# Keys and queries loaded further ahead, and the second layer's weights fetched in quarters, in a fused attention and soft-MoE kernel

## The chip, the cores and the metric

One core of one Trainium2 chip runs the whole kernel. The metric is the device time of one execution in microseconds (us), the median of several runs; lower is better.

## The reference

Three stages follow each other; the result of each is the input of the next. Shapes: q, k, v (4, 8, 1152, 64); phi (512, 32); w1 (8, 512, 1024); w2 (8, 1024, 512); w_in (512, 2048); w_out (2048, 512).

```python
# 1. attention, 4 batches x 8 heads, the queries pooled by pairs
q_pool = q.reshape(B, H, S // 2, 2, D).mean(axis=3)          # 576 queries, 1152 keys
attn = softmax(q_pool @ k.T / sqrt(D)) @ v                   # row sum + 1e-9
x = attn.transpose(0, 2, 1, 3).reshape(2304, 512)
# 2. soft mixture of 8 experts with 4 slots each
logits = x @ phi                                             # 2304 x 32
d = softmax(logits, over tokens); c = softmax(logits, over slots)
slot_out[e] = relu((d.T @ x)[e] @ w1[e]) @ w2[e]
x = c @ slot_out                                             # 2304 x 512, of rank 32
# 3. second layer
h = x @ w_in
g = h where h >= 1, 0 where h <= -1, (h + 1)^2 / 4 between
out = g @ w_out                                              # 2304 x 512
```

## The kernel before, in words

**Attention.** The 32 heads are taken in 16 pairs P, and the 1152 keys of a pair in 9 chunks. One chunk of one pair is a group g = 9P + c, and a group has two slots, one for each head. In each slot TensorE (PE) makes the scores (`st`, L371), ScalarE (ACT) their exponential `e` (L376), PE the product with the values (`acc`, L401), and PE and VectorE (DVE) the row maximum that a later pair needs (`mx` L305, `mp` L317). All other work, such as loading and preparing a later pair, is put into named slots by a table: `plan(P)` calls `at(group, slot, function, ...)`, and the program is written out group after group. Each engine runs its instructions in that order, and so does SP, the queue that issues all DMAs of the stage: an issue that must wait holds up all behind it.

Preparing pair P: `load_k2` and `load_q` fetch keys and queries (`kf` two issues, `qf` four), `prep_khi` (ACT, L252) and `prep_klo` (DVE) split the keys into two f16 parts in `kn`, `prep_qp`, `prep_qhi` and `prep_qlo` pool and split the queries (`qn`), `xpose_k` and `xpose_q1` are DMA transposes into `K1` and `q1`, and `dup_q1` (L291) copies q1 to the other 64 partitions. `qf` has one buffer: a pair's queries can be fetched only when `prep_qlo` of the pair before has read it. The row maxima of pair P are computed on PE (`mx`) from group 9P - 11 on, and they read K1 and q1 with its copy. The places of these steps relative to b = 9P are the two rows of the table `PREP`, in the order load, khi, klo (half groups), qp (half groups), qhi, qlo (half groups):

```python
PREP = (-20, -18, (-34, -33), -36, -16, -30), (-24, -22, (-41, -37), -41, -19, -37)
```

Row 0 is used for P = 2, row 1 for P from 3 on. Between these steps, w_out and w_in are unpacked: a piece is loaded (`f`), turned into `wst` and written to the DRAM copies `wo_dr` and `wi_dr`.

**Mixture.** Logits and softmax over tokens run along with attention. Then 32 tiles of 1 MB with halves of w1 and w2 pass through a ring of buffers on the SP queue: `h` (L775), `ht` (L784, a PE transpose), `s2o` (L827).

**Second layer.** As x = c · slot_out, h is computed as c · M with M = slot_out · w_in (32 rows). M is summed on PE from four tiles `wi`, each with 128 rows of w_in and all 2048 columns (L924). PE multiplies in f32r, so operands are split into a high part (a copy by ACT) and a low part (a subtraction): `Mhi` and `Mlo`, `ghi` and `glo` (GpSimd, which the profile calls POOL), `whi` and `wlo` (L905, L907). `w_split` makes those of w_out, and its subtractions are on POOL for 10 of the 16 row blocks and on DVE for 6. `Mrep` spreads M over the partitions (L948). Then a block of 256 tokens (n) goes through four quarters (qd) of w_in's columns: `h_unit` makes h and clips it (`cl`), `g_unit` forms g in `r`, `g_split` its two parts, and `o_part` multiplies with w_out in 12 matmuls per quarter and half block. For the first block `first_unit` and `o_first` do the same in smaller steps; units are numbered from there.

Of the kernel before, what the change touches and what calls it, by code (L numbers as in the profile page):

```python
# [13 lines left out]
ALU = mybir.AluOpType  # L14
# [18 lines left out]
LGT = 30, 31, 32, 33, 34, 36, 37  # L33
LPT = 6
WPH = 3
REA = 0
# [4 lines left out]
ADD = ((4, 1, 0, 0, 2), (5, 1, 1, 0, 1), (6, 1, 1, 1, 2), (6, 2, 0, 0, 2), (7, 2, 1, 0, 2), (8, 3, 0, 0, 1), (9, 3, 0, 1, 2),  # L41
       (10, 3, 1, 0, 2), (10, 4, 0, 0, 1), (11, 4, 0, 1, 2), (12, 4, 1, 0, 1), (13, 4, 1, 1, 2))

PREP = (-20, -18, (-34, -33), -36, -16, -30), (-24, -22, (-41, -37), -41, -19, -37)


@with_exitstack
def fused_kernel(ctx: ExitStack, tc: tile.TileContext, q, k, v, phi, w1, w2, w_in, w_out, out):
# [59 lines left out]
    wlist += [("wi", dc, 0) for dc in range(4)]  # L108
    wo_dr = dr_p.tile([128, 16, DM], F32, name="wo_dr")
    wi_dr = dr_p.tile([4, 128, DFF], F32, name="wi_dr")  # L110
    wt = {}
    nloaded, gone = 0, set()

    def w_load():
        nonlocal nloaded
        i = nloaded
        nloaded += 1
        kind, e, x = wlist[i]
        if i == NSL:
            t = x_p.tile([128, NTT * DM], F32, tag="xn", name="w1_last")[:, 0:2048]  # L120
        else:
            sl = i if i < NSL else (i - NSL - 1) % NWL
            t = wslot[sl].tile([128, 2048], F32, tag=f"w{sl}", name=f"{kind}_{e}_{x}")
        if kind == "w1":
            src = w1[e, :, x * 512:(x + 1) * 512].rearrange("(c p) f -> p c f", p=128)
            vw = t.rearrange("p (c f) -> p c f", c=4)
        elif kind == "w2":
            src = w2[e, x * 512:(x + 1) * 512, :].rearrange("(c p) d -> p c d", p=128)
            vw = t.rearrange("p (c d) -> p c d", c=4)
        else:  # L130
            src, vw = wi_dr[e], t
        if i < len(wlist) - 1:
            nc.sync.dma_start(out=vw, in_=src)
        else:

            for hf in range(2):
                a, b = [y.rearrange("p (j n) -> p j n", j=4)[:, :, hf * 256:hf * 256 + 256] for y in (vw, src)]
                nc.sync.dma_start(out=a, in_=b)
        wt[kind, e, x] = vw

    def w_used(*keys):
# [51 lines left out]
    def cv_step(n, i):  # L193
        t, dst = cv[n]
        d = dst.bitcast(I32)
        if i == 0:

            nc.vector.tensor_scalar(out=dst, in0=dst, scalar1=CLO, scalar2=CHI, op0=ALU.max, op1=ALU.min)
        elif i == 1:
            nc.vector.tensor_scalar(out=d, in0=d, scalar1=3, scalar2=0x3fffffff,  # L200
                                    op0=ALU.logical_shift_left, op1=ALU.bitwise_and)
        elif i == 2:
            nc.vector.scalar_tensor_tensor(out=d, in0=t[:, :, 1], scalar=-0x40000000, in1=d,
                                           op0=ALU.bitwise_and, op1=ALU.bitwise_or)
# [379 lines left out]
    def plan(P):  # L584
        b = NK * P
        if P > 1:
            lk, hk, lok, aq, hq_, loq = PREP[P > 2]
            for h in range(2):
                at(b + lk, 0, (load_k2, load_q)[h], P)
                at(b + hk, h, prep_khi, P, h)  # L590
                at(b + lok[h] // 2, lok[h] % 2, prep_klo, P, h)
                at(b - 17, h, xpose_k, P, h)
            at(b + aq // 2, aq % 2, prep_qp, P)
            at(b + hq_, 0, prep_qhi, P)
            at(b - 16, 0, xpose_q1, P)
# [58 lines left out]
    with tc.manual_schedule():  # L654
# [126 lines left out]
        def ht_mm(i):  # L781
            htp[i] = sc_tile("ht0")[:, 0, :] if i == 0 else hp_tile("ht1")
            for kc in range(4):
                nc.tensor.transpose(out=htp[i][:, kc * 128:(kc + 1) * 128], in_=h1s[i][:, kc * 128:(kc + 1) * 128],  # L784
                                    identity=ident)
# [24 lines left out]
        def c_xpose(n):  # L810
            for i in range(2):
# [79 lines left out]
        for hl in range(2):  # L891
            for j in range(4):
                for r in range(4):
                    src = ident[:, 32 * j:32 * j + 32] if r // 2 == hl else zcol.to_broadcast([128, 32])
                    nc.gpsimd.tensor_copy(Sel[:, hl, j, 32 * r:32 * r + 32], src)
        for e in range(E_):
            s2o(e, 1)
        pieces = [(0, 2), (2, 4), (4, 8), (8, 12), (12, 16)]
        for f0, f1 in pieces:
            nc.sync.dma_start(out=wlo[:, f0:f1, :].bitcast(F32), in_=wo_dr[:, f0:f1, :])  # L900


        def w_split(f0, f1):
            for f in range(f0, f1):
                nc.scalar.activation(out=whi[:, f, :], in_=wlo[:, f, :].bitcast(F32), func=AF.Copy)  # L905
                eng = nc.gpsimd if f < 4 or f % 2 else nc.vector
                eng.tensor_tensor(out=wlo[:, f, :], in0=wlo[:, f, :].bitcast(F32), in1=whi[:, f, :].bitcast(F32),  # L907
                                  op=ALU.subtract)

        nc.vector.tensor_copy(S2sb, s2)  # L910
        c_xpose(0)
# [4 lines left out]
        Mp = [po_tile(f"M{i}")[:, 0:DM // 2] for i in range(2)]  # L916
        wps = po_tile("warm_o")
        for dc in range(4):
            if dc < 2:
                c_xpose(1 + dc)  # L920
            for i in range(2):
                for j in range(4):
                    c0 = j * 512 + i * 256
                    nc.tensor.matmul(Mp[i][32 * j:32 * j + 32], lhsT=soT[:, dc, :],  # L924
                                     rhs=wt["wi", dc, 0][:, c0:c0 + 256], start=(dc == 0), stop=(dc == 3))
        Mst = x_p.tile([128, NTT * DM], F32R, tag="xn", name="Mst")
        Mhi, Mlo = Mst[:, DFF:DFF + DM], Mst[:, DFF + DM:DFF + 2 * DM]
        HF = [slice(0, DM // 2), slice(DM // 2, DM)]
        for i, sl in enumerate(HF):
            nc.scalar.activation(out=Mhi[:, sl], in_=Mp[i], func=AF.Copy)  # L930
            nc.vector.tensor_tensor(out=Mlo[:, sl], in0=Mp[i], in1=Mhi[:, sl].bitcast(F32), op=ALU.subtract)

        w_split(0, 2)
        wx.close()


        g_p = ctx.enter_context(tc.tile_pool(name="g", bufs=6))
# [3 lines left out]
        NBK = NT // TB  # L941
        ghi, glo, hq = {}, {}, {}

        def Mrep(j, parts):
            for i, sl in enumerate(parts):
                ps = hp_tile(f"Mr{j}_{i}")[:, 0:sl.stop - sl.start]
                for hl, src in enumerate((Mhi, Mlo)):
                    nc.tensor.matmul(ps, lhsT=Sel[:, hl, j, :], rhs=src[:, sl], start=(hl == 0), stop=(hl == 1))  # L948
                dst = Mst[:, j * 512 + sl.start:j * 512 + sl.stop]
                if (i + j) % 2 == 0:  # L950
                    nc.vector.tensor_copy(dst, ps)
                else:
                    nc.scalar.activation(out=dst, in_=ps, func=AF.Copy)


        def h_unit(n, qd, j0, j1):
# [32 lines left out]
        units = [(n, qd, 0, 4) for n in range(NBK) for qd in range(4)][2:]  # L989

        def unit_step(i):
            if i < len(units):
# [58 lines left out]

        pos = o_tiles(0)
        warm_o(WARM[3])
        Mrep(0, HF)
        for f in range(5):
            if f == 4:
                warm_o(WARM[4])
            first_unit(f)
            if f == 1:
                Mrep(1, [slice(0, DM)])  # L1060
                w_split(2, 4)
        nu = 0

        def ahead(n):
            nonlocal nu
# [4 lines left out]
        for n in range(NBK):  # L1070
            if n:
                pos = o_tiles(n)
            if n < NBK - 1:
                for qd in range(4):
                    if n == 0 and qd == 0:
                        for f in range(4):
                            o_first(0, pos, f)
                            if f < 2:
                                first_unit(5 + f)
                                Mrep(2 + f, [slice(0, DM)])  # L1080
                            if f == 1:
                                w_split(4, 8)
                            ahead(FIRST[f])
# [50 lines left out]
```

## Time and profile before

| | before |
|---|---|
| time, median of 3 runs | 782.35 us (782.05 to 782.71) |
| profiled execution, its own time | 787.7 us |
| its span | 785.9 us |
| mean granted TensorE clock | 0.983 |
| PE busy | 757.1 us, 96% |
| DVE busy | 581.4 us, 74% |
| ACT busy | 451.7 us, 57% |
| POOL busy | 125.9 us, 16% |

The page of the profile cuts the span into 40 slices of 19.6 us. Each digit is a busy share in tenths, PEclk is the granted clock in tenths:

```profile
PE   7779999999999999999999999999789999999998
DVE  6878999988989888999988793151697777666520
PEclk8889999999999999999999999999989999999999
DMA  8786788797788797799998836799600000000000
```

PE works in nearly every slice. Its low digits stand at the start (slices 1 to 3) and about two thirds of the way (slices 29 and 30), where the mixture ends and the second layer starts; the clock is below 9 tenths in the same places.

### The profile page before, as it was taken

What the parts mean: (1) busy time and instruction counts of PE and PEld (TensorE: products, weight loads), DVE (VectorE), ACT (ScalarE), POOL (GpSimd) and SP (SyncE); (2) the same over time, 40 slices, a digit from 0 to 9 for tenths busy, and PEclk for the clock granted to TensorE, in tenths of its full rate; (3) what the DMA queues carried; (4) which work ended last, traced back from release to release, by engine and by line L of the source; (5) the groups of instructions that cost most, each with busy time, mean ns of one, the idle gap of its engine ahead of it and who ended that gap; (6) DMA issues with size and microseconds to landing.
All of it is one profiled execution on the core that took longest, in us unless ns stands there. A gap on an engine that the chain in (4) does not pass through costs nothing.

```text
span 785.9 us, 19049 instructions
## 1 busy us (share of the span) xinstructions
PE 757.1 (96%) x7896; PEld 556.6 (71%) x7896; DVE 581.4 (74%) x947; ACT 451.7 (57%) x855; POOL 125.9 (16%) x100
## 2 busy tenths in 40 slices
PE   7779999999999999999999999999789999999998
PEld 6557777766767766777766776633578888888887
DVE  6878999988989888999988793151697777666520
ACT  4246667676657565676675666401686777556620
POOL 7000000000000000000000000002574444443330
PEclk8889999999999999999999999999989999999999
DMA  8786788797788797799998836799600000000000
GB/s 215 201 174 137 182 193 205 206 248 200 186 233 203 183 260 164 188 263 180 212 263 134 222 96 237 269 333 395 241 0 28 28 28 20 7 28 28 27 28 28
DMA packets 138263, 127.11 MB, mean 162 GB/s; under 512 B 80576, under 2 KB 100288, under 8 KB 137408
## 3 DMA queue, kind: packets, MB, share of 16 engines
q1 hardware_dynamic: 138176, 125.89, 61.0%
q8 instruction: 62, 1.02, 0.6%
q14 instruction: 25, 0.20, 0.1%
HBM read 87.10 MB, written 13.11 MB: 128 GB/s over the span
## 4 chain that ended last, share of the span: by engine, by line
PE 60%; DMA 2%; DVE 2%; ACT 2%; issue 1%; SPq 0%; ACTq 0%; DVEq 0%
PE acc L401 9%; PE st L371 9%; PE po L1031 8%; PE po L1032 8%; PE po L1033 8%; PE mx L305 4%; PE acc L394 3%; DMA wi<-wi_dr 2%; PE h L968 2%; PE h L775 2%; PE tx L439 1%; PE tb L466 1%; DVE r L1021 1%; PE tr L428 1%; PE lp L482 0%
## 5 line engine op out<-in xcount | busy, mean ns | idle before, releaser
L376 ACT ACTIVATE e<-st 128x576 f32<-128x576 f32 x288 | 187.0, 651 | 139.0 <-PE st L371 125.6
L317 DVE TENSOR_REDUCE mp<-mx 128x1 f32<-128x576 f32 x282 | 212.1, 754 | 44.9 <-PE mx L305 38.0
L401 PE MATMUL acc<-e,vf 128*64 128x288 f32 x1152 | 195.1, 411 | 0.5 <-ACT e L376 0.5
L305 PE MATMUL mx<-K,q 128*64 128x288 f16 x1152 | 124.8, 298 | 9.6 <-DVE mp L317 3.4
L371 PE MATMUL st<-q,K 128*64 128x288 f16 x1152 | 122.0, 288 | 5.9 <-ACT e L376 4.7
L371 PE MATMUL st<-q,S 128*64 128x288 f16 x1152 | 122.0, 287 | 0.0
L305 PEld LDWEIGHTS <-q 128*64 128x64 f16 x1152 | 66.3, 112 | 70.2 <-issue 24.5
L1031 PE MATMUL po<-whi,ghi 128*128 128x512 f32 (+1 forms) x280 | 108.5, 388 | 0.0
L1032 PE MATMUL po<-wlo,ghi 128*128 128x512 f32 (+1 forms) x280 | 108.5, 388 | 0.0
L1033 PE MATMUL po<-whi,glo 128*128 128x512 f32 (+1 forms) x280 | 108.0, 386 | 0.0
L981 DVE TENSOR_TENSOR r<-cl,r 128x1024 f32<-128x1024 f32 x34 | 80.6, 2372 | 36.9 <-ACT cl L980 36.9
L987 POOL TENSOR_TENSOR glo<-r,ghi 128x1024 fp32r<-128x1024 f32 x34 | 82.2, 2417 | 95.3 <-ACT ghi L986 95.3
L401 PEld LDWEIGHTS acc<-e,vf 128*64 128x64 f32 x1152 | 77.4, 137 | 8.3 <-ACT e L376 2.0
L371 PEld LDWEIGHTS <-K 128*64 128x64 f16 x1152 | 68.3, 110 | 20.9 <-issue 12.7
L752 POOL MEMSET xfer<- 128x1024 f32 x1 | 1.0, 957 | 493.5 <-PE pb L562 493.5
L384 DVE TENSOR_TENSOR es<-es,e 128x288 f32<-128x288 f32 (+1 forms) x144 | 77.5, 550 | 2.2 <-ACT e L376 2.2
L371 PEld LDWEIGHTS <-S 128*64 128x64 f16 x1152 | 69.3, 110 | 3.4
L971 ACT ACTIVATE r<-h,cols 128x512 f32<-128x512 f32 x68 | 43.0, 685 | 31.4 <-PE h L968 31.4
L1033 PEld LDWEIGHTS po<-whi,glo 128*128 128x128 f32 x280 | 53.2, 190 | 10.8
L1031 PEld LDWEIGHTS po<-whi,ghi 128*128 128x128 f32 x280 | 53.4, 191 | 9.8
L1032 PEld LDWEIGHTS po<-wlo,ghi 128*128 128x128 f32 x280 | 53.3, 190 | 9.3
L972 DVE TENSOR_SCALAR cl<-h 128x512 f32<-128x512 f32 x68 | 43.8, 685 | 15.8 <-ACT r L971 13.9
(191 smaller groups left out, 854.1 us busy)
## 6 DMA issues: line engine op xcount, KB each, us to landing
w<-in_moe_w_dram SPq DMA_DIRECT2D x31, 1024.0 KB, 7.9
vf<-in_v_dram SPq DMA_DIRECT2D x16, 576.0 KB, 6.1
kf<-in_k_dram SPq DMA_DIRECT2D x30, 288.0 KB, 4.1
f<-in_moe_w_out_dram SPq DMA_DIRECT2D x16, 512.0 KB, 5.1
f<-in_moe_w_in_dram SPq DMA_DIRECT2D x16, 512.0 KB, 5.5
qf<-in_q_dram SPq DMA_DIRECT2D x30, 256.0 KB, 4.9
S<-K SPq DMA_DIRECT2D x16, 288.0 KB, 5.6
out_dram<-ob SPq DMA_DIRECT2D x17, 256.0 KB, 2.0
```

What stands on the lines that cost most here:

```text
L305: nc.tensor.matmul(ps[p0:p1, i, 0:HQ], lhsT=q1[P][:, t, p0:p1], rhs=kk[:, j * HQ:(j + 1) * HQ], start=True, stop=True)
L317: nc.vector.tensor_reduce(out=mp[P][:, t, a:a + 1], in_=ps[:, :, 0:HQ], op=ALU.max, axis=AX.XY)
L371: nc.tensor.matmul(ps[c0:c0 + 64, i, 0:HQ], lhsT=kk[:, ci, c0:c0 + 64], rhs=f[:, sl[i]], start=first, stop=not first)
L376: nc.scalar.activation(out=e, in_=ps[:, :, 0:HQ], func=AF.Exp, scale=ESC)
L384: nc.vector.tensor_tensor(out=Es[P, n, h][:, i0:i1], in0=a[:, i0:i1], in1=b[:, i0:i1], op=ALU.add)
L401: nc.tensor.matmul(acc[P, i][h * 64:(h + 1) * 64, 0:HQ], lhsT=vt[P][:, h, c, :], rhs=E[P, c, h][:, i, :], start=(c == 0), stop=(c == NK - ...
L972: nc.vector.tensor_scalar(out=cl[:, a:b], in0=src, scalar1=-1.0, scalar2=1.0, op0=ALU.max, op1=ALU.min)
L981: nc.vector.tensor_tensor(out=r[:, sl], in0=cl[:, sl], in1=r[:, sl], op=ALU.add)
L987: nc.gpsimd.tensor_tensor(out=glo[n, qd][:, sl], in0=r[:, sl], in1=ghi[n, qd][:, sl].bitcast(F32), op=ALU.subtract)
L1031: nc.tensor.matmul(po, lhsT=ghi[n, qd][:, j, sl], rhs=whi[:, f, cs], start=(f == 0), stop=False)
L1032: nc.tensor.matmul(po, lhsT=ghi[n, qd][:, j, sl], rhs=wlo[:, f, cs], start=False, stop=False)
L1033: nc.tensor.matmul(po, lhsT=glo[n, qd][:, j, sl], rhs=whi[:, f, cs], start=False, stop=(f == 15))
```

## The change

1. Attention: in row 1 of `PREP` the load stands at -26 instead of -24, and row 1 is used from P = 4 on instead of from P = 3, so P = 3 takes row 0. For P from 4 on, `xpose_k`, `xpose_q1` and `dup_q1` stand one group earlier. Three steps of the logits (`LGT`) stand one half group later.
2. w2 is fetched so that one partition holds four consecutive rows of w2 (an 8 KB piece of DRAM) instead of four rows 128 apart (four pieces of 2 KB); the transposes `ht` read with a stride of four to match.
3. w_in is stored and fetched by quarters of its columns. Quarter 0 goes through the ring; quarters 1 and 2 are loaded into parts of `whi` that are written later, quarter 3 into its own buffer. On SP they alternate with quarters of w_out.
4. M is made one quarter at a time (`M_piece`), a quarter ahead of its use; `Mrep` spreads one quarter, with its two copies on DVE and ACT.
5. All 16 subtractions of `w_split` are on DVE. Two of the three copies to `cT` that ACT made are on DVE.

```diff
-PREP = (-20, -18, (-34, -33), -36, -16, -30), (-24, -22, (-41, -37), -41, -19, -37)
+PREP = (-20, -18, (-34, -33), -36, -16, -30), (-26, -22, (-41, -37), -41, -19, -37)
...
-            lk, hk, lok, aq, hq_, loq = PREP[P > 2]
+            lk, hk, lok, aq, hq_, loq = PREP[P > 3]
...
-                at(b - 17, h, xpose_k, P, h)
+                at(b - 17 - (P > 3), h, xpose_k, P, h)
...
-            at(b - 15, 1, dup_q1, P)
+            at(b - 15 - (P > 3), 1, dup_q1, P)
...
-            src = w2[e, x * 512:(x + 1) * 512, :].rearrange("(c p) d -> p c d", p=128)
+            src = w2[e, x * 512:(x + 1) * 512, :].rearrange("(p c) d -> p c d", p=128)
...
+        for q_ in range(3):
+            if q_:
+                wi_load(q_, whi[:, 4 * q_ + 4:4 * q_ + 8, :].bitcast(F32).rearrange("p f d -> p (f d)"))
+            wo_load(q_)
...
-                eng = nc.gpsimd if f < 4 or f % 2 else nc.vector
-                eng.tensor_tensor(out=wlo[:, f, :], ...
+                nc.vector.tensor_tensor(out=wlo[:, f, :], ...
...
+        def M_piece(q_):
+            ps = hp_tile(f"M{q_}")[:, 0:128]
+            for dc in range(4):
+                for j in range(4):
+                    nc.tensor.matmul(ps[32 * j:32 * j + 32], lhsT=soT[:, dc, :],
+                                     rhs=wt["wi", q_, 0][:, dc, j * 128:(j + 1) * 128], start=(dc == 0), stop=(dc == 3))
+            sl = slice(q_ * 128, (q_ + 1) * 128)
+            nc.scalar.activation(out=Mhi[:, sl], in_=ps, func=AF.Copy)
+            nc.vector.tensor_tensor(out=Mlo[:, sl], in0=ps, in1=Mhi[:, sl].bitcast(F32), op=ALU.subtract)
...
+        def quarter(q_):
+            u, f = (0, q_, 0, 4), 4 * q_
+            Mrep(q_)
+            h_unit(*u)
+            w_split(f, f + 2)
+            g_unit(*u)
+            w_split(f + 2, f + 4)
+            g_split(*u)
...
                         o_part(n, tt, qd, pos[tt])
+                        if n == 0 and qd == 1 and tt == 0:
+                            M_piece(3)
+                            quarter(3)
```

On SP the change moves the loads of pair 4 (`kf_991` and `qf_994` before, `kf_880` and `qf_883` now) past the transposes and the copy of pair 3 (`K_3`, `q_3`). Before, from the first transpose of pair 3's keys on:

```order
L266 DMA_TRANSPOSE K_3_881<-kn_614 128x9x128
L246 DMA vf_904<-in_v_dram 128x2x576
L266 DMA_TRANSPOSE K_3_881<-kn_614 128x9x128
L209 DMA wo_dr<-wst_797 128x512
L185 DMA f_4_909<-in_moe_w_out_dram 128x1024
L288 DMA_TRANSPOSE q_3_939<-qn_105 128x9x128
L229 DMA kf_991<-in_k_dram 128x576 x2
L237 DMA qf_994<-in_q_dram 128x4x128
L238 DMA qf_994<-in_q_dram 128x4x128
L239 DMA qf_994<-in_q_dram 64x128
L240 DMA qf_994<-in_q_dram 64x128
L291 DMA q_3_939<-q_3_939 64x1152
```

The same place now:

```order
L260 DMA_TRANSPOSE K_3_878<-kn_829 128x9x128
L223 DMA kf_880<-in_k_dram 128x576 x2
L231 DMA qf_883<-in_q_dram 128x4x128
L232 DMA qf_883<-in_q_dram 128x4x128
L233 DMA qf_883<-in_q_dram 64x128
L234 DMA qf_883<-in_q_dram 64x128
L240 DMA vf_909<-in_v_dram 128x2x576
L260 DMA_TRANSPOSE K_3_878<-kn_829 128x9x128
L203 DMA wo_dr<-wst_789 128x512
L179 DMA f_4_915<-in_moe_w_out_dram 128x1024
L282 DMA_TRANSPOSE q_3_946<-qn_105 128x9x128
L285 DMA q_3_946<-q_3_946 64x1152
```

The four issues of `qf` stand ahead of five issues that pair 3 needs or that lie between, and the copy `q_3<-q_3` follows its transpose directly.

On DVE, in the first block of the second layer, `cl_2` is the clipped h of quarter 2 and `cl_3` that of quarter 3. Before, from the last step of the second unit on:

```order
L951 CAST Mst<-Mr_0_8682 128x512
L1021 TENSOR_TENSOR r_1_8654<-cl_1_8655,r_1_8654 128x512
L907 TENSOR_TENSOR wlo<-wlo,whi 128x512 x2
L972 TENSOR_SCALAR cl_2_8714<-h_2_0_8715 128x512
L972 TENSOR_SCALAR cl_2_8714<-h_2_1_8720 128x512
L907 TENSOR_TENSOR wlo<-wlo,whi 128x512 x2
L972 TENSOR_SCALAR cl_3_8740<-h_3_0_8741 128x512
L972 TENSOR_SCALAR cl_3_8740<-h_3_1_8746 128x512
```

The same place now (L914 is `w_split`, L938 the low part of a quarter of M, L965 a copy of `Mrep`):

```order
L914 TENSOR_TENSOR wlo<-wlo,whi 128x512 x2
L1033 TENSOR_TENSOR r_1_8665<-cl_1_8666,r_1_8665 128x512
L914 TENSOR_TENSOR wlo<-wlo,whi 128x512 x2
L965 CAST Mst<-Mr_8735 128x256
L984 TENSOR_SCALAR cl_2_8747<-h_2_0_8748 128x512
L984 TENSOR_SCALAR cl_2_8747<-h_2_1_8753 128x512
L914 TENSOR_TENSOR wlo<-wlo,whi 128x512 x2
L993 TENSOR_TENSOR r_2_8746<-cl_2_8747,r_2_8746 128x1024
L914 TENSOR_TENSOR wlo<-wlo,whi 128x512 x2
L938 TENSOR_TENSOR Mst<-M_8784,Mst 128x128
L965 CAST Mst<-Mr_8803 128x256
L984 TENSOR_SCALAR cl_3_8815<-h_3_0_8816 128x512
```

Between `cl_2` and `cl_3` stood two subtractions of w_out; now there stand four, the sum of g of quarter 2, the low part of the last quarter of M and a copy of it.

## Rows read from the trace of the kernel before

**Rows 1.** Windows: stretch and length, each engine's busy us, PEclk, DMA, GB/s.

```profile
46.60:65.30 18.70, 14.78 (x176) 10.71 (x177) 11.47 (x23) 7.24 (x12) 0.00 (x0) 0.82 0.48 117
52.87:59.69 6.82, 5.79 (x46) 3.78 (x46) 3.89 (x8) 2.99 (x5) 0.00 (x0) 0.50 0.35 66
65.30:76.50 11.20, 11.20 (x158) 8.07 (x156) 10.94 (x20) 6.78 (x15) 0.00 (x0) 1.00 0.92 187
...
516.00:545.70 29.70, 29.55 (x272) 8.79 (x272) 12.43 (x46) 2.04 (x3) 5.24 (x33) 1.00 1.03 382
545.70:572.40 26.70, 20.14 (x162) 13.94 (x158) 16.52 (x28) 16.39 (x35) 13.85 (x12) 0.99 0.61 241
...
572.40:587.50 15.10, 15.04 (x58) 12.38 (x59) 14.22 (x15) 12.39 (x19) 12.63 (x7) 0.80 0.00 0
```

**Rows 2.** Timeline, ACT and PE, 46 to 55 us: start, length, what, [idle before <-releaser].

```profile
51.04 0.68 ACT L252 ACTIVATE kn<-kf 128x576 f16<-128x576 f32 x1 [3.07 <-DMA kf<-in_k_dram]
...
52.31 0.44 PE L371 MATMUL st<-q,K 128*64 128x288 f16 x4 [2.88 <-ACT e L376]
```

**Rows 3.** Timeline, SP's queue and PE, 71 to 87 us.

```profile
71.56 0.54 SPq L246 DMA_DIRECT2D vf<-in_v_dram  x1
...
75.10 2.62 SPq L288 DMA_TRANSPOSE q<-qn  x1
...
78.86 0.43 SPq L237 DMA_DIRECT2D qf<-in_q_dram  x1
...
81.63 0.53 SPq L291 DMA_DIRECT2D q<-q  x1
...
86.34 0.41 PE L305 MATMUL mx<-K,q 128*64 128x288 f16 x4
```

**Rows 4.** DMA issues at 71, 46.5 (two), 435.8, 27: KB each, us to landing.

```profile
q<-qn SPq DMA_TRANSPOSE x1, 6.3
...
q<-q SPq DMA_DIRECT2D x1, 144.0 KB, 5.8
...
qf<-in_q_dram SPq DMA_DIRECT2D x2, 256.0 KB, 6.8
...
q<-q SPq DMA_DIRECT2D x1, 144.0 KB, 2.2
...
qf<-in_q_dram SPq DMA_DIRECT2D x2, 256.0 KB, 4.1
```

**Rows 5.** Timeline, PE, the three longer waits between 200 and 300 us.

```profile
231.35 0.44 PE L305 MATMUL mx<-K,q 128*64 128x288 f16 x4 [0.72 <-DMA q<-q]
...
261.06 0.44 PE L305 MATMUL mx<-K,q 128*64 128x288 f16 x4 [1.76 <-issue]
...
288.40 0.70 PE L401 MATMUL acc<-e,vf 128*64 128x288 f32 x2 [0.52 <-ACT e L376]
```

**Rows 6.** Timeline, PE, POOL and DVE, 548 to 577 us.

```profile
548.32 1.07 PE L924 MATMUL M<-wi,soT 128*32 128x256 f32 x16
...
553.60 0.64 PE L924 MATMUL M<-wi,soT 128*32 128x256 f32 x8 [0.84 <-DMA wi<-wi_dr]
...
555.80 2.52 POOL L907 TENSOR_TENSOR wlo<-wlo,whi 128x512 fp32r<-128x512 f32 x2 [11.83 <-ACT whi L905]
...
556.06 0.42 DVE L1015 TENSOR_SCALAR cl<-h 128x256 f32<-128x256 f32 x1 [0.48 <-PE h L1014]
...
557.06 1.53 DVE L1021 TENSOR_TENSOR r<-cl,r 128x256 f32<-128x256 f32 x1
...
564.27 0.70 DVE L1021 TENSOR_TENSOR r<-cl,r 128x512 f32<-128x512 f32 x1
564.89 0.68 DVE L1025 TENSOR_SCALAR r<-h 128x512 f32<-128x512 f32 x1
...
571.73 1.28 DVE L972 TENSOR_SCALAR cl<-h 128x512 f32<-128x512 f32 x2
...
576.41 1.21 DVE L981 TENSOR_TENSOR r<-cl,r 128x1024 f32<-128x1024 f32 x1
```

More of the change, by code (lines that the diff above doesn't have):

```diff
@@ L107, in fused_kernel @@
     wlist.insert(NSL, LASTW)
-    wlist += [("wi", dc, 0) for dc in range(4)]
+    wlist += [("wi", 0, 0)]
     wo_dr = dr_p.tile([128, 16, DM], F32, name="wo_dr")
-    wi_dr = dr_p.tile([4, 128, DFF], F32, name="wi_dr")
+    wi_dr = dr_p.tile([128, 4, 4, 512], F32, name="wi_dr")
     wt = {}
@@ L127, in w_load @@
         elif kind == "w2":
-            src = w2[e, x * 512:(x + 1) * 512, :].rearrange("(c p) d -> p c d", p=128)
+            src = w2[e, x * 512:(x + 1) * 512, :].rearrange("(p c) d -> p c d", p=128)
             vw = t.rearrange("p (c d) -> p c d", c=4)
         else:
[L131 to L138, printed above, removed]
+            src, vw = wi_dr[:, e], t.rearrange("p (c n) -> p c n", c=4)
+        nc.sync.dma_start(out=vw, in_=src)
         wt[kind, e, x] = vw
@@ L783, in ht_mm @@
             for kc in range(4):
[L784 to L785 removed]
+                nc.tensor.transpose(out=htp[i][:, kc * 128:(kc + 1) * 128],
+                                    in_=h1s[i].rearrange("p (n k) -> p k n", k=4)[:, kc, :], identity=ident)
         def ht_sum(i):
@@ L915, in fused_kernel @@
         po_p = ctx.enter_context(tc.tile_pool(name="po", bufs=4, space=PS))
-        Mp = [po_tile(f"M{i}")[:, 0:DM // 2] for i in range(2)]
+        for n in (1, 2):
+            c_xpose(n)
         wps = po_tile("warm_o")
[L918 to L925, printed above, removed]
         Mst = x_p.tile([128, NTT * DM], F32R, tag="xn", name="Mst")
         Mhi, Mlo = Mst[:, DFF:DFF + DM], Mst[:, DFF + DM:DFF + 2 * DM]
[L928 to L933, printed above, removed]
+        def M_piece(q_):
[7 more added lines that the diff above has]
+            nc.vector.tensor_tensor(out=Mlo[:, sl], in0=ps, in1=Mhi[:, sl].bitcast(F32), op=ALU.subtract)
+        M_piece(0)
         wx.close()
+        wi3_p = ctx.enter_context(tc.tile_pool(name="wi3", bufs=1))
+        wi_load(3, wi3_p.tile([128, 2048], F32, name="wi3"))
+        wo_load(3)
         g_p = ctx.enter_context(tc.tile_pool(name="g", bufs=6))
@@ L942, in fused_kernel, with Mrep @@
         ghi, glo, hq = {}, {}, {}
-        def Mrep(j, parts):
-            for i, sl in enumerate(parts):
-                ps = hp_tile(f"Mr{j}_{i}")[:, 0:sl.stop - sl.start]
+        def Mrep(q_):
+            ps = hp_tile(f"Mr{q_}")
+            for j in range(4):
                 for hl, src in enumerate((Mhi, Mlo)):
[L948 to L951, printed above, removed]
+                    nc.tensor.matmul(ps[:, j * 128:(j + 1) * 128], lhsT=Sel[:, hl, j, :], rhs=src[:, q_ * 128:(q_ + 1) * 128],
+                                     start=(hl == 0), stop=(hl == 1))
+            for i in range(2):
+                c0, sl = q_ * 512 + i * 256, slice(i * 256, i * 256 + 256)
+                if i:
+                    nc.scalar.activation(out=Mst[:, c0:c0 + 256], in_=ps[:, sl], func=AF.Copy)
                 else:
-                    nc.scalar.activation(out=dst, in_=ps, func=AF.Copy)
+                    nc.vector.tensor_copy(Mst[:, c0:c0 + 256], ps[:, sl])
         def h_unit(n, qd, j0, j1):
@@ L987, in g_split @@
             nc.gpsimd.tensor_tensor(out=glo[n, qd][:, sl], in0=r[:, sl], in1=ghi[n, qd][:, sl].bitcast(F32), op=ALU.subtract)
-        units = [(n, qd, 0, 4) for n in range(NBK) for qd in range(4)][2:]
+        units = [(n, qd, 0, 4) for n in range(NBK) for qd in range(4)][4:]
         def unit_step(i):
@@ L1053, in fused_kernel @@
         warm_o(WARM[3])
[L1054 to L1057, printed above, removed]
+        Mrep(0)
+        M_piece(1)
+        for f in range(4):
             first_unit(f)
-            if f == 1:
-                Mrep(1, [slice(0, DM)])
-                w_split(2, 4)
+            if f < 2:
+                w_split(2 * f, 2 * f + 2)
+        Mrep(1)
         nu = 0
+        def quarter(q_):
[6 more added lines that the diff above has]
+            g_split(*u)
         def ahead(n):
@@ L1077, in fused_kernel @@
                             o_first(0, pos, f)
[L1078 to L1083, printed above, removed]
+                            if f < 3:
+                                first_unit(4 + f)
+                            if f == 0:
+                                M_piece(2)
+                            elif f < 3:
+                                w_split(2 * f + 2, 2 * f + 4)
+                        quarter(2)
                         continue
-                    if n == 0 and qd < 3:
-                        w_split(4 * qd + 4, 4 * qd + 8)
-                    ahead(4 * n + qd + AHEAD + min(n, RUN))
+                    if n or qd > 1:
+                        ahead(4 * n + qd - 2 + AHEAD + min(n, RUN))
                     for tt in range(2):
                         o_part(n, tt, qd, pos[tt])
+                        if n == 0 and qd == 1 and tt == 0:
+                            M_piece(3)
+                            quarter(3)
                         if qd == 3:
```

23 lines of the change are left out of this document (14 added, 9 removed).

## The prediction

> **What bounds the kernel now.** I read the page's slices first, for places where PE is not full, then windows around them, then the timeline of each place, and last the order of the queues that feed it.
>
> PE is the bound nearly everywhere. Three places lose time.
>
> The first is in attention, at 46.6 us. The window holds 18.70 us and PE works for 14.78, so 3.9 us are idle; behind the wait the granted clock is 0.50, the lower level of 1.2 GHz, for 6.82 us in which PE is busy 5.79 [rows 1]. At 2.4 GHz that work takes half, so the low clock costs 2.9 us. The cause stands in the timeline: ACT waits 3.07 us for the keys `kf` of pair 3, and PE 2.88 us for the exponential behind it in ACT's order [rows 2]. The stretch thus loses 3.9 + 2.9 = 6.8 us.
>
> The second is a set of waits in later pairs: 0.72 us for the copy `q<-q`, 1.76 us at the same instruction in a later pair, and 0.52 us behind a late key load [rows 5], together 3.0 us.
>
> The third is the change to the second layer. Between 545.70 and 572.40 us PE works 20.14 of 26.70 us. The last M matmuls wait 0.84 us for w_in and end at 553.60 + 0.64 = 554.24; the first clip on DVE is at 556.06 and the clip of quarter 2 at 571.73 [rows 6]. From then PE is full, 15.04 of 15.10 us, at a mean clock of 0.80 [rows 1]: two fifths of it, 6.0 us, at the lower level, which costs 3.0 us. Just ahead of that PE had been idle in parts. Before 545.70 PE is full (29.55 of 29.70 us), so no transfer there can give more than 0.15 us.
>
> **The change part by part.**
>
> *Keys of pair 3 at -20.* Its load moves from group 3 to group 7, its keys' ACT step to group 9. With the load gone from this place, ACT has nothing to wait for at 51.04, and the stall goes with its low clock: -6.8 us up to the next dependence. That is the first `mx` of pair 3 at 86.34 [rows 3], which would be due at 86.34 - 6.8 = 79.5.
>
> *What it brings: pair 4 passes pair 3 on SP.* Pair 4's load is at group 36 - 26 = 10, the transposes of pair 3 at 10 and 11, its copy at 12. The four `qf` issues of pair 4 wait until DVE's `prep_qlo` of pair 3, in group 12, has read the one `qf` buffer. Behind them on SP stand the values, half the keys' transpose, a write and a load of weights, the query transpose and the copy, all of pair 3's time; the copy is what `mx` needs. When can `prep_qlo` end? Pair 3's load is due at group 7, some 52.5 us (46.6 and two groups of 3 us; two successive pairs reach the same instruction at 231.35 and 261.06, so nine groups take 29.7 us with their waits [rows 5]); the key issues take about 1 us, and the larger query pieces land 4.1 to 6.8 us after issue [rows 4]: 57.7 to 60.4. I take 60.0, as this stretch is as loaded as the one of the 6.8. From `prep_qp`, which needs them, to `prep_qlo` there are 20 DVE instructions; a stretch with 20 took 11.20 us at 10.94 busy [rows 1]. So 71.2 us. Then the four issues, 81.63 - 78.86 = 2.8 less the gap to the copy, 2.5; from the values' issue to the query transpose's 75.10 - 71.56 = 3.5; its landing 6.3; the copy 2.2 alone or 5.8 in company [rows 3, 4]. With 2.2 that is 14.5 us: the copy lands at 85.7, 6.2 us late. PE idles, and as a 2.9 us wait was followed by the lower clock before, I charge the same 2.9 us again. Sum for the beginning: -6.8 + 6.2 + 2.9 = +2.3. Bounds: queries at 57.7 give -0.4 with the low clock (wait 3.5); a copy of 5.8 gives +5.9; with no wait at all it is -6.8.
>
> *Pairs from 4 on, loads two groups and transposes one group earlier.* A group lasts some 3 us, the waits were 0.5 to 1.8 us. All three go: -3.0. If the queue gives the time back elsewhere it is 0. In these pairs, too, `qf` of the next pair stands ahead of the copy, but `prep_qlo` there stands at -37 half groups, 1.5 groups before that load (9 - 26 = -17 groups); in pair 3 it stands two groups behind it.
>
> *w2 by longer rows.* The transfers are off the path (0.15 us at most). The strided read of two groups of four transposes costs between nothing and a doubling of each, 1.2 us by an estimate of 0.15 us per transpose, from PE's 1.07 us for sixteen 256-column matmuls [rows 6] upwards. I take 0.1.
>
> *The second layer.* M's first quarter needs only a quarter of w_in, which lands before PE gets there. PE reaches M at 548.32 [rows 6]; a group of transposes now comes first (0.8, estimate), then sixteen narrower matmuls (1.07 at most): 550.2. From M to the first clip it took 556.06 - 554.24 = 1.8; M's second quarter, now between, adds 0.8. So the first clip is at 552.8, 3.3 us earlier than before.
>
> From there to the clip of quarter 2 DVE took 571.73 - 556.06 = 15.7 us. In the new order six more subtractions of w_out stand between these two places, each 0.62 us (two-input instructions of this size are issued 564.89 - 564.27 apart, rows 6), and small copies worth 0.4: +4.1, so 19.8 us and 572.6 if DVE loses as much to waits as before. That loss is about 5.1 us: 12 instructions at 0.42 and 9 at 0.62 make 10.6. POOL's part of w_split is gone, but the chain DVE, ACT, DVE, PE is as long, so I keep the loss whole.
>
> Then comes what the order adds: between the clips of quarters 2 and 3, DVE does four subtractions (2.5), the sum of g (1.21, rows 6) and the clips themselves (1.2), and only then `Mlo` of the last quarter; with 0.8 us for two-input work beside GpSimd's `glo` it is at 572.6 + 5.7 = 578.3. PE has just half an `o_part` pair (12 matmuls) to cover that. Behind it PE must do the spreading (0.9), wait for a copy (0.4), do h (0.5), and the rest of what filled 15.10 us before: 15.1 - 3.0 = 12.1 us at full clock, of which 36 of 48 matmuls are left, 9.0. End at 578.3 + 10.8 = 589.1 against 587.5: +1.6. That supposes that no low clock falls on this part, as PE had enough to do until 575; it has one before, so this is the kindest assumption, and the third rival gives it up. For the waits of DVE I take the whole loss; with none it would be -3.5.
>
> *Contention.* The first `r` sum of 256 columns, 1.53 us, starts while GpSimd subtracts and ends at 558.59, just behind GpSimd's end at 558.32; the sum of 512 columns took 0.70 [rows 6]. The Trainium skill ("SBUF — State Buffer", section "SBUF: two separate sides") says that a DVE instruction with two SBUF inputs and a GpSimd instruction that reads SBUF lock each other out for the whole instruction. The row agrees: the DVE work seems to run after GpSimd's. By that rule DVE's extra subtractions are no way out of the lock, as `glo` stays on GpSimd: four of 256 and two of 512 columns before quarter 2, at 1.26 us for 512 [rows 6], can hold DVE up by 5.0 us, about the loss taken whole above. Without the lock the second rival would be the likelier.
>
> **Sum.** +2.3 - 3.0 + 0.1 + 1.6 = +1.0 us on the profiled execution's 787.7 (its span is 785.9 and 1.8 lie around it). That execution is 5.3 us above the median of the runs; I put the difference on the median: 782.35 + 1.0 = 783.4 us.
>
> **Rivals.**
>
> 1. *The wait on SP is short or absent.* For it: DVE works 10.94 of 11.20 us in a stretch without a stall's slack, and 20 instructions elsewhere take less; against it: the order of SP has nothing that breaks the chain. Without wait the beginning gives -6.8, in all -8.1, 774.3 us; with 2 us and no low clock 776.3. Chance 0.17.
> 2. *DVE keeps up.* POOL's long subtractions are gone and w_in is early. The loss of 5.1 us goes: `Mlo` at 552.8 + 14.7 + 4.9 = 572.4, the end at 583.2, -4.3 for the second layer, in all -4.9: 777.5 us. Against it: the waits in the first block came from ACT and PE as well. Chance 0.20.
> 3. *Slower: the lower clock moves to where PE is full.* If PE waits for `Mlo` of the last quarter by over 2.9 us, the length of the wait that was followed by the low clock at 52.87, the low stretch falls on the 36 matmuls that follow: +3.0 us, 786.4 us. For it: PE's cover there is 12 matmuls, under 5 us even at half clock. Against it: before, the low stretch ended by itself, and here it may be over by then. Chance 0.20.
> 4. That the change doesn't do what it says at the beginning, because the wait of pair 3 is only carried to another place, is part of the forecast itself.
>
> **How the numbers follow.** The forecast has 0.43, with a range of its own from 781 to 786 (beginning -0.4 to +4, second layer within 1 us). Rivals: 0.17, 0.20, 0.20. Up to 0.2%, or 1.6 us either way, counts as no change for this kernel: 780.8 to 783.9. Faster: rival 1 whole, 0.17 of rival 2 and 0.03 of the forecast, 0.37. The same: 0.26 of the forecast and 0.03 of rival 2, 0.29. Slower: 0.14 of the forecast and rival 3, 0.34. The range of 776.8 to 787.2 leaves out the half of rival 1 without any wait and the ends of rivals 2 and 3, about 0.2.
>
> **What would show it.** Right: no idle ACT before `kn` near 51 us and no half clock at 53; a PE idle of 4 to 7 us at the first `mx` of pair 3, named as waiting for `q<-q`, with SP's `qf` issues late before it and PEclk 0.5 behind it; no waits of that kind in pairs from 4 on; first clip about 3 us earlier, the clip of quarter 3 later than that of quarter 2 by 6 us and more. Wrong: a full PE from 46 to 93 us (rival 1), `cl` of quarter 2 before 569 us by the shifted clock of the second layer (rival 2), or PEclk of 0.5 while `o_part` runs without gaps past its first 12 matmuls (rival 3). A new wait in a stage not named here, above all for `qf` in pairs from 5 on, would make the sum wrong as well.

## The result, and the profile after

| | before | changed |
|---|---|---|
| median | 782.2 us (4 runs, 781.37 to 782.71) | 792.93 us (4 runs, 792.31 to 794.48) |
| ratio | | 1.0136, 95% interval 1.0118 to 1.0155 |
| profiled execution, its span | 787.7, 785.9 us | 794.48, 792.7 us |

The changed kernel is 10.7 us slower. The forecast was 783.4 us, with 787.2 as its upper end; the measured time is 9.5 us above the forecast. Two terms of its sum failed, of similar size. The stall at 46.6 us was put at 6.8 us, and a second execution shows 2.4. In the second layer the step from the first clip to the clip of quarter 2 was put at 19.8 us and took 23.5, and the stage lost 6.9 us where 1.6 were forecast. The two profiled executions differ by 6.8 us only, so the first mistake cannot be seen by laying these two traces side by side.

Attention first. The windows of the changed kernel (length, then PE, PEld, DVE, ACT and POOL busy, then granted clock, DMA share, GB/s) answer to [rows 1]:

```profile
46.60:65.30 18.70, 18.61 (x274) 14.25 (x272) 15.43 (x30) 10.76 (x21) 0.00 (x0) 1.00 0.66 167
87.91:91.32 3.41, 3.19 (x38) 2.16 (x42) 1.09 (x2) 0.65 (x1) 0.00 (x0) 0.50 0.35 68
545.70:572.40 26.70, 19.89 (x192) 15.67 (x188) 16.81 (x34) 11.55 (x26) 4.47 (x5) 0.87 0.51 210
558.95:565.77 6.82, 4.59 (x39) 3.03 (x38) 5.11 (x13) 3.32 (x8) 2.44 (x3) 0.50 0.05 18
572.60:579.42 6.82, 3.63 (x11) 3.06 (x12) 4.36 (x7) 4.52 (x9) 1.27 (x1) 0.50 0.00 1
```

The stall at 46 to 65 us is gone (PE 18.61 of 18.70 us, full clock). A new stretch at the lower level stands at 87.91, and there are two in the second layer, where there had been one. The timeline shows how the first comes about, and answers to [rows 2, 3]:

```profile
53.88 1.05 SPq L223 DMA_DIRECT2D kf<-in_k_dram  x2
...
66.72 0.84 SPq L223 DMA_DIRECT2D kf<-in_k_dram  x2
...
71.56 0.75 DVE L277 SCALAR_TENSOR_TENSOR qn<-qf,qn 128x576 f16<-128x576 f32 x1
72.34 0.38 SPq L231 DMA_DIRECT2D qf<-in_q_dram  x1
...
74.59 0.51 SPq L240 DMA_DIRECT2D vf<-in_v_dram  x1
...
78.08 1.41 SPq L282 DMA_TRANSPOSE q<-qn  x1
...
85.65 0.50 SPq L285 DMA_DIRECT2D q<-q  x1
...
88.13 0.69 PE L299 MATMUL mx<-K,q 128*64 128x288 f16 x4 [4.68 <-issue]
```

Read it downwards. The keys of pair 4 are issued at 66.72 and end at 67.56; SP then issues nothing until 72.34, because `prep_qlo` of pair 3 (L277) runs only at 71.56. Everything that stands behind the four `qf` issues comes 4.8 us late, the transpose is issued at 78.08, lands 7.6 us later, and the copy at 85.65 lets PE go at 88.13 after 4.68 us idle.

The second layer, as the timeline of the changed kernel shows it (answers to [rows 6]):

```profile
553.86 0.42 DVE L1027 TENSOR_SCALAR cl<-h 128x256 f32<-128x256 f32 x1
...
555.38 1.29 DVE L914 TENSOR_TENSOR wlo<-wlo,whi 128x512 fp32r<-128x512 f32 x2 [0.77 <-ACT whi L913]
...
557.91 0.73 PE L1052 MATMUL po<-whi,ghi 128*128 128x512 f32 x2 [2.07 <-ACT ghi L1034]
...
562.20 0.79 PE L1026 MATMUL h<-cT,Mst 128*128 128x256 f32 x2 [2.23 <-DVE Mst L965]
...
569.70 1.00 PE L958 MATMUL Mr<-Mst,Sel 128*128 128x128 f32 x8
...
572.27 0.63 ACT L1034 ACTIVATE ghi<-r 128x512 fp32r<-128x512 f32 x1 [2.11 <-DVE r L1033]
572.81 1.13 ACT L913 ACTIVATE whi<-wlo 128x512 fp32r<-128x512 f32 x2
573.45 1.94 DVE L914 TENSOR_TENSOR wlo<-wlo,whi 128x512 fp32r<-128x512 f32 x2 [1.22 <-ACT whi L913]
575.32 0.41 DVE L965 CAST Mst<-Mr 128x256 fp32r<-128x256 f32 x1
575.78 1.23 PE L980 MATMUL h<-cT,Mst 128*128 128x256 f32 x4 [5.08 <-DVE Mst L965]
577.34 1.29 DVE L984 TENSOR_SCALAR cl<-h 128x512 f32<-128x512 f32 x2 [1.61 <-ACT r L983]
...
582.51 0.29 DVE L938 TENSOR_TENSOR Mst<-M,Mst 128x128 fp32r<-128x128 f32 x1
...
594.27 0.64 PE L980 MATMUL h<-cT,Mst 128*128 128x256 f32 x4
```

Quarter 2's o matmuls are over at 594.27; the same instruction stood at 587.35 before, so this stage costs 6.9 us:

```profile
587.35 0.64 PE L968 MATMUL h<-cT,Mst 128*128 128x256 f32 x4
```

The largest piece is PE's 5.08 us at 575.78. It waits for a copy of 0.41 us. The matmuls that the copy reads (L958) were done at 570.7; the copy stands on DVE behind two subtractions that wait for ACT's `whi`, which stands on ACT behind a `ghi` that waits for DVE's sum.

The mixture begins at nearly the same time in both first traces, that of the kernel before and that of the changed one:

```profile
516.00 1.49 PE L775 MATMUL h<-w,xfer 128*32 128x512 f32 x12 [0.45 <-DVE xfer L767]
...
516.04 1.50 PE L769 MATMUL h<-w,xfer 128*32 128x512 f32 x12 [0.45 <-DVE xfer L761]
```

If the trace of the kernel before is typical, attention has neither lost nor gained.

### The profile page after: what moved, and what is told of

It is laid out like the page before. It is cut to its first block, busy times and chain, and to the rows that moved or that the text cites. A ratio compares the mean times of both kernels' runs of the same rounds, so it can differ in the third digit from the quotient of the medians.

```text
span 792.7 us, 19223 instructions
## 1 busy us (share of the span) xinstructions
PE 759.1 (96%) x7974; PEld 560.6 (71%) x7974; DVE 581.1 (73%) x964; ACT 450.4 (57%) x855; POOL 109.3 (14%) x90
## 4 chain that ended last, share of the span: by engine, by line
PE 83%; DVE 6%; DMA 4%; ACT 3%; SPq 1%; issue 1%; ACTq 0%; DVEq 0%
PE st L365 17%; PE acc L395 16%; PE mx L299 9%; PE po L1044 8%; PE po L1043 8%; PE po L1045 8%; PE acc L388 5%; PE h L980 2%; DVE mp L311 2%; PE tx L433 2%; DMA wlo<-wo_dr 2%; DMA q<-qn 1%; PE tb L460 1%; ACT e L370 1%; DMA qf<-in_q_dram 1%
## 5 line engine op out<-in xcount | busy, mean ns | idle before, releaser
L993 DVE TENSOR_TENSOR r<-cl,r 128x1024 f32<-128x1024 f32 x34 | 78.3, 2304 | 37.6 <-ACT cl L992 37.6
```

What stands on the lines that cost most here:

```text
L993: nc.vector.tensor_tensor(out=r[:, sl], in0=cl[:, sl], in1=r[:, sl], op=ALU.add)
```

## Experiments

Each run was timed beside the kernel before on the same chip; ratios are to that kernel, with 95% intervals.

**1. The kernel before, profiled again.** No edit.

> The kernel before, once more with a profile, because its first profiled execution took 787.7 us against a median of 782.2, while the changed kernel's profiled execution is only 1.6 us above its median. Theory A (the first trace shows a loss that most executions don't have): a span near 780.5 us, and either the idle time near 50 us with its low clock (6.8 us) or the low clock at 572 to 578 us (3 us) is missing. Theory B (the trace is typical): a span near 785 us with both.

Measured: one execution of 783.16 us, span 781.4. Its timeline and the same window as above:

```profile
49.85 0.68 ACT L252 ACTIVATE kn<-kf 128x576 f16<-128x576 f32 x1 [1.60 <-DMA kf<-in_k_dram]
...
51.12 0.44 PE L371 MATMUL st<-q,K 128*64 128x288 f16 x4 [1.42 <-ACT e L376]
...
54.76 0.44 PE L305 MATMUL mx<-K,q 128*64 128x288 f16 x4 [1.00 <-DMA q<-q]
...
511.50 1.49 PE L775 MATMUL h<-w,xfer 128*32 128x512 f32 x12 [0.45 <-DVE xfer L767]
```

```profile
46.60:65.30 18.70, 16.21 (x245) 11.74 (x242) 15.51 (x29) 9.94 (x18) 0.00 (x0) 1.00 0.52 128
```

The wait for pair 3's keys is there, but PE loses 1.42 + 1.00 = 2.4 us and the clock stays at 2.4 GHz. In the first trace it lost 3.9 us and 2.9 us more by the clock. The mixture begins at 511.50 instead of 516.00, which is the 4.5 us between the two spans. Laid side by side by the exponentials of the same group, the two traces part by 4.0 us between groups 5 and 8, in this stretch; the rest is small differences in later pairs. Theory A holds: the stall that the forecast took away costs 2.4 us in this execution, not 6.8. A third trace with the same attention (experiment 3) has waits of 2.00 and 0.52 us there, no fall of the clock, and the mixture at 509.51. Of the 66 timed executions of the kernel before that these runs hold, one (787.26 us) comes near the 787.7 us of the first profiled one.

**2. Attention part alone, second layer as before.** The changes of `PREP`, of the three transposes and copies that follow it, and of `LGT`, on the kernel before.

> The kernel before with the attention part of the change alone (PREP, LGT, transposes a group earlier). In the two traces the start of the mixture moved by +0.04 us, gain at pair 3 and loss behind it cancelling. If those traces are typical: within 1 us of 782.2. If the stall near 50 us of the kernel before is missing in most of its executions (theory A), the gain is not there and the new wait of 4.65 us with its low clock stays: 785 to 789 us.

Measured: 787.92 us, ratio 1.0079 (1.005 to 1.0108). The mixture begins at 516.61; PE waits at pair 3's first `mx`:

```profile
86.23 0.44 PE L305 MATMUL mx<-K,q 128*64 128x288 f16 x4 [3.40 <-issue]
...
516.61 1.48 PE L775 MATMUL h<-w,xfer 128*32 128x512 f32 x10 [0.45 <-DVE xfer L767]
```

The wait of 4.68 us in the changed kernel is 3.40 us here, so its length differs between executions. The attention part loses 5.6 us by the medians, and its mixture begins 5.1 us later than in experiment 1, as theory A had it.

**3. Second layer (and w2) alone, attention as before.**

> The changed kernel with the attention part taken back, so w2 by long rows and the second layer in quarters alone. The end of the first block's quarter 2 moved from 587.35 to 594.27 us, +6.9, and the mixture did not move: 789 us if the tail holds all of the loss that the traces show; 792 to 793 us if the tail holds the whole measured difference; the rest of it, if any, then lies in attention.

Measured: 788.41 us, ratio 1.0084 (1.0057 to 1.0111).

```profile
51.45 0.44 PE L365 MATMUL st<-q,K 128*64 128x288 f16 x4 [2.00 <-ACT e L370]
...
509.51 1.49 PE L769 MATMUL h<-w,xfer 128*32 128x512 f32 x12 [0.45 <-DVE xfer L761]
```

Its mixture begins at 509.51, and from there to the end of its span of 786.1 it takes 276.6 us; in the changed kernel that is 792.7 - 516.0 = 276.7, and in the two traces of the kernel before 785.9 - 516.0 = 269.9 and 781.4 - 511.5 = 269.9. The second layer's loss is thus the same with either attention. The two losses, 5.6 and 6.1 us, sum to 11.7 against 10.7 measured together: each part of the change loses, and within the intervals they add. The change of w2 was in no run alone; it is in this one.

**4. Pair 4's load behind pair 3's copy.**

```diff
-                at(b + lk, 0, (load_k2, load_q)[h], P)
+                at(b + (-23 if P == 4 else lk), 0, (load_k2, load_q)[h], P)
```

> The changed kernel with pair 4's key and query loads at group 13 instead of 10, behind the copy of pair 3 on SP. If the wait of pair 3 comes from the four query issues held on SP: the 4.65 us wait at 83 us and the low clock at 88 us are gone, and all later groups start 5 to 7 us earlier, 786 to 788 us. If the copy is late for another reason (the query transpose itself, or DVE's prep being late): the wait stays above 3 us, and the time within 1.5 us of 792.9. If pair 4 is now late itself, a wait of some us appears near group 25.

Measured: 787.93 us, ratio 1.0073 (1.0047 to 1.0098), 5.0 us less than the changed kernel. On SP the copy now goes at 75.34, 10 us earlier, and the queries of pair 4 follow it:

```profile
75.34 0.49 SPq L285 DMA_DIRECT2D q<-q  x1
75.89 1.07 SPq L223 DMA_DIRECT2D kf<-in_k_dram  x2
77.47 0.39 SPq L231 DMA_DIRECT2D qf<-in_q_dram  x1
...
508.72 1.50 PE L769 MATMUL h<-w,xfer 128*32 128x512 f32 x12 [0.45 <-DVE xfer L761]
```

PE has no wait above 0.3 us at pair 3 or near group 25, and the mixture begins 7.3 us earlier than in the changed kernel. That is more than the 5.0 us between the medians: the profiled execution of the changed kernel is 1.55 us above its median, and this one 0.5 below its own. That is the wait, named and removed: four issues on SP held by one buffer.

**5. The same with the second layer as before.** The edits of 2 and 4 on the kernel before.

> The kernel before with the attention part of the change and pair 4's load at group 13, the second layer as before. In the changed kernel with that load the mixture began at 508.27 us against 511.05 in the second trace of the kernel before: 2.8 us less, 779.4 us. If moving pair 4 alone does not repair the attention part (theory: the attention loss of 5.6 us has another cause): 785 to 788 us.

Measured: 781.69 us, ratio 0.9985 (0.9968 to 1.0002): no difference that this measurement can tell, where 779.4 was expected. The mixture began at 511.02 in its trace. Two waits that the trace of experiment 4 does not have came up here (0.93 us at 199.69 us and 1.24 at 346.75; the trace of experiment 2 has them too, with 0.46 and 1.53). With its own wait mended, the attention part neither gains nor loses by more than this measurement can tell. That fits a removed stall of about 2.4 us and not of 6.8, less such waits, which some traces with this attention have and others not.

**6. Copies of the spread M ahead of the subtractions.** On experiment 4. Quarter 1's spreading moves up from behind the loop, quarter 2's out of `quarter(2)`:

```diff
             first_unit(f)
+            if f == 1:
+                Mrep(1)
             if f < 2:
                 w_split(2 * f, 2 * f + 2)
-        Mrep(1)
...
                             elif f < 3:
+                                if f == 1:
+                                    Mrep(2)
                                 w_split(2 * f + 2, 2 * f + 4)
```

> The changed kernel with pair 4's load at group 13 (787.9 us) and, in the second layer, the copies of the spread M of quarters 1 and 2 ahead of the subtractions of w_out in DVE's and ACT's order. Theory order (h waits for a copy that stands behind subtractions): PE's waits of 1.4 to 2.2 and 5.1 us at h are gone, 781.5 to 783.5 us. Theory load (DVE and ACT have too much to do between the first clip and quarter 2, whatever the order): the waits move to the next o matmuls, 786 us or more.

Measured: 784.45 us, ratio 1.0021 (1.0005 to 1.0038), 3.5 us less than experiment 4 and just above the range of theory order. PE's waits at h of 5.1 and 1.4 us are gone. A part came back as a wait of 3.07 us before the spreading of the last quarter:

```profile
571.17 1.42 PE L958 MATMUL Mr<-Mst,Sel 128*128 128x128 f32 x8 [3.07 <-ACT Mst L937]
```

**7. The last quarter of M up as well.** `M_piece(3)` before `quarter(2)`, its spreading directly behind quarter 2's h.

> As the one before, and M's last quarter and its spreading also ahead of quarter 2's subtractions. Theory order: another 1 to 1.5 us less than that one (waits of 0.45 and 0.52 us and part of the lower clock behind them). Theory load: the same time within 0.7 us, as PE waits for the high and low parts anyway.

Measured: 781.85 us, ratio 0.9987 (0.9968 to 1.0006), another 2.6 us less, more than the 1 to 1.5 us of theory order. The order alone thus gives back 6.1 us, as much as the second layer had lost in experiment 3. From the mixture's start to the end the trace takes 269.3 us, as short as the kernel before (269.9), though this execution is 1.8 us below its median. The timeline shows what is left:

```profile
550.81 1.22 PE L1052 MATMUL po<-whi,ghi 128*128 128x512 f32 x2 [2.79 <-ACT ghi L1034]
...
564.30 0.33 PE L958 MATMUL Mr<-Mst,Sel 128*128 128x128 f32 x1 [1.37 <-ACT Mst L937]
565.79 1.00 PE L958 MATMUL Mr<-Mst,Sel 128*128 128x128 f32 x7 [1.17 <-DVE Mst L938]
```

```profile
550.60:554.00 3.40, 3.19 (x8) 2.49 (x8) 2.43 (x6) 2.04 (x6) 0.73 (x1) 0.50 0.39 157
565.30:587.00 21.70, 20.92 (x105) 17.57 (x106) 18.16 (x25) 18.07 (x28) 7.20 (x3) 1.00 0.04 14
```

In this execution the clock falls only at 550.60, and the stretch behind 565.30, where PE is full, is at full speed.

**8. The subtractions shared with GpSimd as before.** On experiment 4, copies where the change put them:

```diff
-                nc.vector.tensor_tensor(out=wlo[:, f, :], ...
+                eng = nc.gpsimd if f < 4 or f % 2 else nc.vector
+                eng.tensor_tensor(out=wlo[:, f, :], ...
```

> The changed kernel with pair 4's load at group 13 (787.9 us) and the subtractions of w_out shared as before, 10 on GpSimd and 6 on DVE. If the move to DVE made the loss: back by 4 us or more, 784 us or less. If the order of the copies made it (they stay behind ACT's whi and the subtractions that are left on DVE): within 1.5 us of 787.9. If the lock between DVE and GpSimd costs more than the move: slower, 788.5 to 791.

Measured: 785.89 us, ratio 1.0032 (1.0016 to 1.0048), 2.0 us less than experiment 4: between the two theories. The wait at h stays almost whole:

```profile
549.09 0.73 PE L1053 MATMUL po<-whi,ghi 128*128 128x512 f32 x2 [0.79 <-ACT ghi L1035]
551.57 1.22 PE L1053 MATMUL po<-whi,glo 128*128 128x512 f32 x2 [1.30 <-POOL glo L1036]
...
566.62 1.23 PE L981 MATMUL h<-cT,Mst 128*128 128x256 f32 x4 [4.94 <-DVE Mst L966]
```

So the move to VectorE costs something at the first o matmuls, but the place of the copies costs more, whichever engine subtracts.

**9 and 10. Experiment 7 with four, or ten, of the subtractions on GpSimd.**

> The changed kernel with pair 4's load at group 13, all spread copies of M ahead of the subtractions (781.9 us), and the subtractions of the first four row blocks of w_out on GpSimd as in the kernel before. What is left there is PE's wait of 2.79 us at the first o matmul, for a sum on DVE that stands behind two subtractions. Theory order: most of that wait goes, 1.0 to 2.5 us less, 779.4 to 780.9, which is faster than the kernel before. Theory lock (GpSimd's subtractions hold up DVE's sums for as long): within 0.7 us of 781.9.

> As the one before, with the whole sharing of the kernel before (10 blocks on GpSimd, 6 on DVE). With the copies no longer behind the subtractions, theory order gives no further gain: within 0.8 us of best2. Theory load gives 1 to 2 us less than best2, as in the step from 787.9 to 785.9 us.

Measured: 781.41 us, ratio 0.9979 (0.9962 to 0.9996), and 781.33 us, ratio 0.998 (0.9967 to 0.9992). Both intervals end below 1: these two are a little faster than the kernel before, by about 0.2%. Against experiment 7, best2 gains only 0.4 us, within what theory lock expected, and best3 no more. In best2's trace PE's wait for `ghi` falls to 1.52 us, and 0.92 us for `glo` on GpSimd comes in its place.

Experiments 4, 7, 8 and 10 together are the four combinations of the two orders with the two ways of sharing the subtractions. Moving the copies ahead gives 6.1 us with all subtractions on DVE (787.93 to 781.85) and 4.6 with the shared ones (785.89 to 781.33). Sharing gives 2.0 us with the copies behind the subtractions and 0.5 with the copies ahead.

## Why the prediction was wrong

**The first term was read from one execution and carried to the median.** The forecast said that the stretch at 46.6 us "thus loses 3.9 + 2.9 = 6.8 us". It noted that the profiled execution was 5.3 us above the median, and carried the change reckoned from it to the median all the same. Experiment 1 shows that 4.0 of the 4.5 us between the spans of the two executions lie in this stretch: the second half of the keys lands 6.4 us after its issue and not 3.8, PE waits longer, and the clock falls. The other two traces with this attention, one of them 0.8 us from the median, do not have it. With 2.4 us in place of 6.8, the forecast's own beginning is -2.4 + 6.2 + 2.9 = +6.7 instead of +2.3, and the sum 787.8. The 5.3 us should have been asked for its place before any of the idle time was counted as a gain.

**The new wait on SP was right.** `prep_qlo` was forecast to end at 71.2 us and ended at 72.31; the copy was forecast to land at 85.7, and PE went on at 88.13 (the transpose took 7.6 us in place of 6.3). PE reached the place at 83.4 instead of 79.5. Of its lead of 5.9 us at group 8, 4.5 were left at group 14, and the trace of experiment 4 loses as much there; pair 3's work on DVE and ACT now stands in these groups (32 and 33 instructions in place of 30 and 31), which is argued as the cause and not tested. Another 0.74 us went at 81.53, which the forecast had not seen: an exponential stands on ACT behind a step of pair 4's keys, and this waits 1.34 us for the half of the keys' transpose that the four issues had held on SP. So the wait at the copy was 4.68 us and not 6.2, and the low stretch 3.41 us long, with 3.19 us of PE work, which costs 1.6 us and not 2.9:

```profile
80.25 0.68 ACT L246 ACTIVATE kn<-kf 128x576 f16<-128x576 f32 x1 [1.34 <-DMA K<-kn]
...
81.53 0.46 PE L395 MATMUL acc<-e,vf 128*64 128x288 f32 x1 [0.74 <-ACT e L370]
```

In all, the distance between the two traces went from -5.94 at group 8 to +3.30 at group 18, by 9.2 us; the forecast had -6.8 to +2.3, by 9.1. The mechanism was right. That the sizes agree so well is partly luck, since several of its parts were off in opposite directions. Experiment 4 removes these two waits, and the earlier loss of lead stays. A slip in the bounds: with the queries at 57.7 in place of the 60.0 taken, the wait would be 3.9 us and the sum 0.0, not 3.5 and -0.4.

**The later pairs.** -3.0 us was forecast; from group 18 to the mixture the two first traces moved by 3.26 us, and the three waits are gone. In the second trace of the kernel before the three are 0.51, 0.57 and 0.43, so half of the 3.0 belongs to the first execution as well.

**w2 by longer rows.** 0.1 us was put down; a strided transpose takes 310 ns on average in place of 286, eight of them, so 0.2 us in all. The term holds, as far as this row goes.

**The second layer was mis-sized, at one step.** Up to the first clip the working held to 1.1 us: 552.8 forecast, 553.86 measured. The step that failed is "From there to the clip of quarter 2": 15.7 + 4.1 = 19.8 us forecast, 577.34 - 553.86 = 23.5 measured. I had added the subtractions' durations to a stretch as if DVE's order had only become longer. But a copy of 0.41 us on which PE waits was now behind them, and each pair of subtractions waits for ACT, which in its own order waits for DVE. That "the chain DVE, ACT, DVE, PE is as long" was the assumption that failed: the copy had joined it. Experiments 6 and 7 move only copies and M's last quarter, no work, and give 6.1 us. The end was forecast 1.6 us later and came 6.9 later; of the missing 5.3 us 1.1 are the later first clip and 3.7 this step. Behind it, `Mlo` of the last quarter was due 5.7 us after the clip of quarter 2 and came at 582.51, 5.2 after it, and what then follows took 11.8 us where 10.8 were put down. Of ACT's copies to `cT`, three of six moved to DVE, and not two of three as the list of the change says.

**The rivals.** The third, the low clock falling on full PE work, came only in part. Its condition, a long wait for `Mlo` of the last quarter, did not come: PE waited 0.56 us there. The second low stretch, 572.60 to 579.42, holds PE work of 3.63 us only, and all of PE's work behind it ran at full clock. What it misjudged is that the clock fell twice and earlier: at 558.95, 1.0 us behind a wait of 2.07 us, and at 572.60, inside the wait of 5.08 us. Rival 1 is refuted by the wait of 4.68 us and by experiment 4, rival 2 by the clip of quarter 2 at 577.34, which it had before 569. The third rival's cover of 12 matmuls, "under 5 us even at half clock", is 6.0 us by the forecast's own 9.0 us for 36, and 5.1 us by the 0.43 us between those that ran in the low stretch.

**Contention.** With GpSimd's `glo` beside it, the pair of subtractions at 573.45 took 1.94 us, and the pair at 555.38 without it 1.29:

```profile
572.98 1.27 POOL L1035 TENSOR_TENSOR glo<-r,ghi 128x512 fp32r<-128x512 f32 x1 [2.49 <-ACT ghi L1034]
```

By the rule that the prediction cites from the Trainium skill ("SBUF — State Buffer", section "SBUF: two separate sides") the second instruction waits for the first to end. The trace agrees: GpSimd ends at 574.25, and the first subtraction of the pair, 0.69 us long when alone, ends at 574.79. But the price here is 0.65 us, not the 5.0 taken as the rule's upper bound, and experiment 8 put GpSimd's subtractions back and came out faster, so the lock does not decide this stage.

What stays open: why the keys came late in the first profiled execution of the kernel before. Timed executions of it spread from 779.92 to 787.26 us. In all three traces with this attention a 16 KB load on the instruction queue starts at 50.9 to 51.0 us, and a pause of 2.2 to 3.2 us follows in the landings of SP's loads. In the first trace the second half of the keys, issued 0.7 us later than in the second (47.78 and 47.05), falls into this pause and lands at 54.16; in the other two it had landed by 50.94, and the pause falls on a load of queries. That this load makes the pause was not tried.

## What to carry to other kernels

Where a profiled execution stands far from the median, find the place of the difference before counting any of its idle time as a gain: profile the same kernel again. When a load is moved ahead in an in-order queue, look for the one buffer it needs; a held issue delays all that stands behind it, here by 4.8 us, and the cure is its place in the queue. When work is added to an engine, ask what small instruction others wait for is now behind it: a 0.41 us copy behind four subtractions and a sum cost PE 5 us.

## What the runs showed of the hardware

In the kernel before, PE's wait of 2.88 us that ended at 52.31 was followed by the lower clock at 52.87; at the same place of two other executions waits of 1.42 and 1.00 us, and of 2.00 and 0.52 us, were not. In the second layer of the changed kernel a wait of 2.07 us that ended at 557.91 was followed by it at 558.95. Transfers of 1 MB with 8 KB pieces landed 2.5 us apart in the mixture of the changed kernel, against 2.7 us with 2 KB pieces in the kernel before, with the queue full in both.
